# A thirteenth 8 KiB tile, w1's sums by 640 columns, and each head's gK one iteration earlier in a one-core attention block with its gradients

## The chip, the core and the metric

The kernel runs on one core of one Trainium2 chip. The metric is the device time of one execution in microseconds (us), the median of the runs. The engines are TensorE (PE in the profile; PEld is its weight load), VectorE (DVE), ScalarE (ACT), GpSimd (POOL) and SyncE (SP). SP issues the loads, POOL the stores of the two big gradients, ScalarE the stores of the weights' gradients; all of them move over the same 16 DMA engines.

## The reference

One decode step of a transformer block for 2 batch rows, and its gradients. B = 2, D = 640, 32 heads of 128, a cache of 4096 keys and values, a hidden width of 1728. All tensors are bf16.

```python
x1 = layernorm(x);  q = x1 @ wq                      # (B, 32, 128)
p  = softmax(q @ k^T * 128**-0.5);  o = p @ v        # per batch row and head, 4096 keys
h  = x + o @ wo;  x2 = layernorm(h)
out = h + relu(x2 @ w1) @ w2
# returned: out, and for a given grad_out the gradients of
# x, k_cache, v_cache, wq, wo, w1, w2
```

The caches are 64 MiB each, and so are their gradients. For each pair of batch row and head, the gradient of v (gV) is the outer product of p (4096) and the gradient of o (128); the gradient of k (gK) is the outer product of the scores' gradient and q. The scores' gradient needs dp = v times the gradient of o, so V is needed again after the whole forward pass of its batch row.

## The kernel before, in words

**Tiles.** A K or V tile of one head is 128 partitions by 8 KiB, 1 MiB. `NBIG = 12` such tiles (L80) are shared out by tag: "ld" for loads, "g" for gV and gK, "f" and "q" for later work. `take` and `give` (L89, L105) hand them out in order; `share` (L118) says how many each tag shall own. A load waits, on SP, until the last reader of the tile it takes over is done, and the loads behind it on SP wait with it. The queue of loads (L1100 to L1129) is filled in order: K of head i, V of head i - 2, later W (V for the second pass), with w1, w2 and wo between them; `pump` issues as many as there are free tiles.

**First pass.** `p1_iter(i)` (L449) works on three heads at once, in eight steps k = 0 to 7. For head i: K is transposed on TensorE (as pairs of bf16 in fp32, L423), copied to SBUF by ScalarE (L428, tiles "XT", five buffers) and multiplied by q (L436). For head i - 1: the maximum (rmax L559, spread by a product L503, reduced to nb L505), the exponential (ep, L512, its sum in `es`), and two halves of pk, K weighted by ep (L464, VectorE). For head i - 2: V weighted by the probabilities (m_ps, L457, 32 products) and a row of u (L486). The last six V tiles of batch row 0 and of batch row 1 are kept (`KEPT`, L395) for the second pass.

**Middle of a batch row.** `middle_gen(b)` (L719) runs in the background, some steps per iteration: the layer norm, the hidden layer, and the gradient that comes back. Through w1 it comes as sums of products on VectorE (`ttr`, L641, w1_t times a row spread over all partitions, `fbc`, into a scratch row `junk`): three stretches of 576 columns for each of 5 chunks, 15 sums. `bcast_cols` (L615) spreads the row, 512 columns at a time, by TensorE and a copy on ScalarE. `go_group` (L658) then forms, for up to eight heads, the gradient of o by one sum over wo_t each, and what else the heads need. `turn()` (L649) lets one sum go ahead for each place that `slot` grants.

**Second pass.** `p2_iter(j)` (L814) does head j: transposes W (tiles T0 to T3), forms dp; spreads two rows by products (L831) that ScalarE copies to `rb`; POOL copies the probabilities to `pp`; VectorE forms gV in two halves (L809) from rb and pp, POOL stores it (L871). The last quarter of dp, the scores' gradient gsp (L822) and gK (two halves at L809, stored at L850) of head j are done at the start of `p2_iter(j + 1)`.

**Order.** The plan (L1089 to L1097) runs first-pass iterations 0 to 33, then 34 to 40 beside the middle of batch row 0. From iteration 41 (`P2_AT`) to 63 every second one also runs a second-pass head; I call it heavy and the one between light. A heavy iteration takes five steps of `p2_iter` after steps k = 1, 1, 3, 4 and 6 of the first pass (`MIXED`, L1139), the light one takes the last, gV's second half with its store, after k = 1 (`REST`, L1140). From iteration 66 on only the second pass runs (heads 14 to 63), with the middle of batch row 1, the gradients of w2, w1, wo and wq (`fin_gen`) and of x (`gx_gen`) in the background. In the mixed iterations the sums have a place after k = 6, and in the light one also after k = 1 (L1217). When two pools are released, more 8 KiB tiles are made in their places.

Of the kernel before, what the change touches and what calls it, by code (L numbers as in the profile page):

```python
# [7 lines left out]
FP32 = mybir.dt.float32  # L8
# [7 lines left out]
def kernel(  # L16
# [63 lines left out]
    NBIG = 12  # L80
# [71 lines left out]
    neg_ident = const.tile([128, 128], BF16)  # L152
    nc.vector.tensor_scalar(out=neg_ident[:], in0=ident_bf[:], scalar1=-SCALE, scalar2=None, op0=ALU.mult)
# [25 lines left out]
    xr = cols.tile([4 * ND, 128], BF16)  # L179
# [96 lines left out]
    def ln_bwd(gh, xh, rstd, add, dst, nb):  # L276

        def t3(name):
            return small.tile([128, nb, ND], FP32, tag=f"lb_{name}{nb}", bufs=1, name=f"lb_{name}")
# [3 lines left out]
        mm = small.tile([128, 2, nb], FP32, tag=f"lb_mm{nb}", bufs=1, name="lb_mm")  # L283
# [5 lines left out]
        nm = small.tile([128, 2, nb], FP32, tag=f"lb_nm{nb}", bufs=1, name="lb_nm")  # L289
# [32 lines left out]
    pkp = tc.alloc_tile_pool(name="pkp", bufs=1)  # L322
    hot = pkp.tile([128, 2 * H - 1], BF16)
    nc.gpsimd.memset(hot[:], 0.0)
    nc.gpsimd.memset(hot[:, H - 1:H], 1.0)
    es = pkp.tile([128, B, H], FP32)
# [73 lines left out]
    u4 = cols.tile([128, 128], FP32)  # L400
# [14 lines left out]
    def pair_transpose(nat, g, dve=False, busy=0):  # L415
# [8 lines left out]
        t_sb = mats.tile([128, GT // 2, 128], FP32, tag="XT", bufs=5, name="t_sb")  # L424
# [24 lines left out]
    def p1_iter(i, dve_group, busy):  # L449
# [60 lines left out]
        if p is not None:  # L510
            ep = pkp.tile([128, NSC, 2], BF16, tag="ep", bufs=3, name="ep")
            nc.scalar.activation(out=ep[:], in_=p["s"][:, :, None].to_broadcast([128, NSC, 2]),  # L512
                                 func=ACT.Exp, bias=nb[:], scale=SCALE, accum_out=es[:, bp, hp:hp + 1])
            p["ep"] = ep
            p["pk"] = []
            pk_tile(0)
# [21 lines left out]
        if p is not None and hp % OG == OG - 1:  # L538

            totp = p["bank"][:, 256:256 + OG]  # L540
            nc.tensor.matmul(totp, lhsT=half_f32, rhs=es[:, bp, hp + 1 - OG:hp + 1], start=True, stop=True)
# [66 lines left out]
    def u_out(b):  # L608

        t = pst([128, H], FP32, "mid", "uc_ps")  # L610
        nc.tensor.matmul(t[:], lhsT=u4[:], rhs=fold[:], start=True, stop=True)
        nc.vector.tensor_tensor(out=Uc[:, b, :], in0=t[:], in1=rt[:, b, :], op=ALU.mult)


# [18 lines left out]
    def store_row(col_bf, n, dst):  # L633
# [3 lines left out]
        r = small.tile([16, 128], BF16, tag="orow", bufs=2, name="orow")  # L637
# [3 lines left out]
    def ttr(in0, in1, acc, width, kc=128, junk=None):  # L641
        if junk is None:
            junk = cols.tile([128, D], BF16, tag="junk", name="junk")
# [14 lines left out]
    def go_group(b, h0, h1, hbc):  # L658
# [4 lines left out]
        for k in range(n):  # L663
            yield from turn()
            ttr(wo_t[:, h0 + k, :], hbc[:], go32[:, k:k + 1], D)
# [25 lines left out]
    def mlp_out():  # L691

        ml32 = small.tile([128, ND, B], FP32, tag="ml32", bufs=1, name="ml32")
# [16 lines left out]
        ml_bf = small.tile([128, ND, B], BF16, tag="ml_bf", bufs=1, name="ml_bf")  # L710
        nc.vector.tensor_copy(out=ml_bf[:], in_=ml32[:])
        y_bf = small.tile([128, B, ND], BF16, tag="y_bf", bufs=1, name="y_bf")
# [6 lines left out]
    def middle_gen(b):  # L719
        if o_next[0] < (b + 1) * H // OG:  # L720
            o_group()
        nc.vector.tensor_reduce(out=u4[:], in_=u_bank[0][:].rearrange("p (s d) -> p d s", s=4),
# [32 lines left out]
        fbc = cols.tile([128, Dff], BF16, tag="fbc", name="fbc")  # L755
# [17 lines left out]
        hbc = cols.tile([128, D], BF16, tag="rowbc", name="hbc")  # L773
        yield from bcast_cols(one(gh1c, b), ND, lambda c: 128, hbc)
# [5 lines left out]
        for h0, h1 in bounds:  # L780
            yield from go_group(b, h0, h1, hbc)
# [3 lines left out]
    def ga_gen():  # L785

        gbc = cols.tile([128, Dff], BF16, tag="fbc", name="gbc")
# [479 lines left out]
```

## Time and profile before

| | us |
|---|---|
| median of 3 runs | 897.68 (895.79 to 898.74) |
| the profiled execution | 897.56 |
| its span, first to last instruction | 895.8 |
| busy: TensorE, VectorE, ScalarE, POOL | 739.5, 687.7, 482.6, 202.7 |

In the span 211.11 MB were read from HBM and 149.13 MB written. The page divides the span in 40 slices of 22.4 us; for each it gives the GB/s moved, and the TensorE clock that was granted as a share of full speed. A view by windows gives the same for any stretch, with each engine's busy time and its count of instructions. A view of waits says which engine waited for whom: us in total, times, the longest. In the timeline the bracket at the end of a row is the idle time before it and what ended it. Matmuls are pipelined and their ends are modelled, so a busy TensorE isn't one at its peak.

### The profile page before, as it was taken

The page shows a single profiled execution, that of the slowest core. Times are in us where ns is not written, and L with a number is a line of the kernel's source. Part 1 is how long each engine was busy: PE and PEld are TensorE (multiplying, and loading weights), DVE is VectorE, ACT ScalarE, POOL GpSimd, SP SyncE. Part 2 cuts the span into 40 slices and gives each one's busy share as a digit, 9 for nine tenths or more (in the row PEclk, how much of TensorE's full clock was granted, in tenths as well). Part 3 has the DMA queues.
Part 4 walks back from the last instruction along what each step waited for, and adds up shares of the span by engine and source line. Part 5 has one row for each costly group of instructions (what it writes and reads, how often), then busy time and mean ns, then how long its engine had stood idle before and what let it go on. Part 6 is the DMA issues. An engine that isn't in the chain of part 4 may idle for free.

```text
span 895.8 us, 24578 instructions
## 1 busy us (share of the span) xinstructions
PE 739.5 (83%) x10145; PEld 616.0 (69%) x10145; DVE 687.7 (77%) x1284; ACT 482.6 (54%) x1242; POOL 202.7 (23%) x349
## 2 busy tenths in 40 slices
PE   4999899899997997997977776877878897787593
PEld 4888788788886886886766765665657665564452
DVE  2666788777887786786877897788788679987963
ACT  1444344344554554564645777777556864466372
POOL 1343444343211110010021232222111111111111
PEclk9999999999999899897995556555566855575555
DMA  9999999999879999999999999999999999999997
GB/s 379 425 418 416 417 406 418 425 424 380 311 307 370 377 399 424 424 424 422 399 383 400 422 419 422 419 415 421 417 417 363 425 425 425 425 425 426 425 422 295
DMA packets 56288, 361.84 MB, mean 404 GB/s; under 512 B 5680, under 2 KB 11760, under 8 KB 15472
## 3 DMA queue, kind: packets, MB, share of 16 engines
q1 hardware_dynamic: 34520, 211.13, 57.9%
q0 software_dynamic: 18432, 134.23, 35.9%
q10 hardware_dynamic: 3224, 14.92, 4.0%
q8 instruction: 80, 1.31, 0.5%
q14 instruction: 32, 0.26, 0.1%
HBM read 211.11 MB, written 149.13 MB: 402 GB/s over the span
## 4 chain that ended last, share of the span: by engine, by line
PE 42%; DMA 28%; DVE 14%; ACT 9%; issue 5%; SPq 1%; POOL 0%; ACTq 0%; POOLq 0%; DVEq 0%
PE t_ps L423 18%; DMA Vt<-in_A_v_cache_dram 13%; PE m_ps L457 10%; DMA out_dram<-gK 9%; DVE gV L809 4%; ACT gV L870 3%; PE s_ps L436 3%; PE u_ps L486 3%; ACT t_sb L428 2%; PE dp_ps L436 2%; DVE gK L809 2%; DVE pk L464 2%; PE o_ps L909 2%; DMA out_dram<-gV 2%; DVE junk L644 2%
## 5 line engine op out<-in xcount | busy, mean ns | idle before, releaser
L428 ACT COPY t_sb<-t_ps 128x512 f32<-128x512 f32 x479 | 273.6, 586 | 194.7 <-PE t_ps L423 189.7
L436 PEld LDWEIGHTS <-t_sb 128*128 128x128 bf16 x4096 | 179.4, 102 | 60.5 <-ACT t_sb L428 30.4
L423 PE MATMUL t_ps<-ident_f,Wt 128*128 128x128 f32 x832 | 197.1, 386 | 2.7 <-DMA Wt<-in_A_v_cache_dram 2.4
L457 PE MATMUL m_ps<-pk,Vt 128*128 128x129 bf16 x2048 | 171.9, 222 | 16.6 <-DMA Vt<-in_A_v_cache_dram 16.0
L464 DVE TENSOR_TENSOR pk<-Kt,ep 128x2048 bf16<-128x2048 bf16 x128 | 156.5, 1223 | 33.5 <-PE m_ps L457 15.4
L809 DVE TENSOR_TENSOR gK<-rb,gsp 128x2048 bf16<-128x2048 bf16 x128 | 152.6, 1226 | 15.3 <-DMA out_dram<-gV 13.2
L423 PE MATMUL t_ps<-ident_f,Kt 128*128 128x128 f32 x1024 | 156.0, 285 | 5.7 <-DMA Kt<-in_A_k_cache_dram 5.5
L423 PEld LDWEIGHTS t_ps<-ident_f,Wt 128*128 128x128 f32 x832 | 137.0, 200 | 32.3 <-issue 25.6
L457 PEld LDWEIGHTS <-Vt 128*128 128x128 bf16 x2048 | 125.3, 99 | 47.7 <-issue 28.9
L809 DVE TENSOR_TENSOR gV<-rb,pp 128x2048 bf16<-128x2048 bf16 (+1 forms) x128 | 142.7, 1140 | 10.2 <-DMA out_dram<-gK 8.8
L474 POOL COPY pk<-ep 128x16 bf16<-128x16 bf16 x80 | 84.1, 1053 | 160.8 <-ACT ep L512 86.5
L423 PEld LDWEIGHTS t_ps<-ident_f,Kt 128*128 128x128 f32 x1024 | 113.2, 145 | 9.8 <-PE s_ps L436 4.1
L436 PE MATMUL dp_ps<-gom,t_sb 128*128 128x2 bf16 x2048 | 95.9, 168 | 20.5 <-ACT t_sb L428 20.3
L871 POOL DMA_DIRECT2D out_dram<-gV x64 | 34.2, 534 | 293.2 <-DVE gV L809 173.5
L436 PE MATMUL s_ps<-qm,t_sb 128*128 128x2 bf16 x2048 | 87.4, 164 | 1.5 <-DVE t_sb L426 1.5
L850 POOL DMA_DIRECT2D out_dram<-gK x64 | 34.0, 531 | 227.6 <-DVE gK L809 172.6
L571 ACT CAST MT<-m_ps 128x128 bf16<-128x128 f32 x64 | 17.1, 267 | 105.3 <-PE m_ps L457 105.1
L915 ACT CAST ot<-o_ps 128x512 bf16<-128x512 f32 (+3 forms) x152 | 68.0, 492 | 6.9 <-DMA out_dram<-ot 5.6
L822 DVE SCALAR_TENSOR_TENSOR gsp<-dp_ps,negdot,P_bf 128x64 bf16<-128x64 f32 x64 | 18.0, 281 | 55.8 <-PE dp_ps L436 55.7
L836 ACT ACTIVATE rb<-dp_ps,rt 128x256 bf16<-128x256 f32 x64 | 30.2, 471 | 56.9 <-PE dp_ps L831 56.8
L644 DVE CUSTOM_DVE_ANT_0 junk<-wo_t,hbc 128x640 bf16<-128x640 bf16 x64 | 52.5, 820 | 0.2
L644 DVE CUSTOM_DVE_ANT_0 gxj<-wqs,gqr 128x1024 bf16<-128x1024 bf16 x40 | 48.8, 1219 | 1.4 <-DMA wqs<-in_A_wq_dram 1.2
(200 smaller groups left out, 763.2 us busy)
## 6 DMA issues: line engine op xcount, KB each, us to landing
Kt<-in_A_k_cache_dram SPq DMA_DIRECT2D x64, 1024.0 KB, 16.5
Vt<-in_A_v_cache_dram SPq DMA_DIRECT2D x64, 1024.0 KB, 16.0
out_dram<-gV POOLq DMA_DIRECT2D x64, 1024.0 KB, 13.5
out_dram<-gK POOLq DMA_DIRECT2D x64, 1024.0 KB, 13.7
Wt<-in_A_v_cache_dram SPq DMA_DIRECT2D x52, 1024.0 KB, 12.0
wq_t<-in_A_wq_dram SPq DMA_DIRECT2D x5, 1024.0 KB, 11.9
wo_t<-in_A_wo_dram SPq DMA_DIRECT2D x4, 1280.0 KB, 19.0
wqs<-in_A_wq_dram SPq DMA_DIRECT2D x5, 1024.0 KB, 21.0
```

The costliest lines, as they stand in the source:

```text
L423: nc.tensor.transpose(t_ps[:, j, :], natf[:, 2 * cc:2 * cc + 2, :].rearrange("p c k -> p (c k)"), ident_f[:])
L428: nc.scalar.copy(out=t_sb[:], in_=t_ps[:])
L436: nc.tensor.matmul(dst[:, sc:sc + 2], lhsT=v[:, j, :, par], rhs=vecs[:, par, :], start=(par == 0), stop=(par == 1))
L457: nc.tensor.matmul(r["m"][:, 0:129], lhsT=r["V"][:, sc, :], rhs=r["pk"][sc // HALF][:, sc % HALF, 0:129], start=(sc == 0), stop=(sc == NSC ...
L464: nc.vector.tensor_tensor(out=p["pk"][k][:, :, 0:128].rearrange("p s (a two) -> p s a two", two=2), in0=p["K"][:, sl, :].rearrange("p s (a ...
L474: nc.gpsimd.tensor_copy(out=col, in_=e)
L644: nc.vector.tensor_tensor_reduce(out=junk[0:kc, 0:width], in0=in0, in1=in1, scale=1.0, scalar=0.0, op0=ALU.mult, op1=ALU.add, accum_out=acc)
L809: nc.vector.tensor_tensor(out=pairs_view(dst[:, sl, :]), in0=row.rearrange("p (a two) -> p a two", two=2)[:, None, :, :].to_broadcast([128 ...
L836: nc.scalar.activation(out=rb[:], in_=bank[:, 128:384], func=ACT.Copy, scale=rt[:, b, h:h + 1])
L850: nc.gpsimd.dma_start(out=natural(out_2, bp, hp), in_=gK[:])
L871: nc.gpsimd.dma_start(out=natural(out_3, b, h), in_=gV[:])
L915: nc.scalar.copy(out=ot[0:P, k, n0:n0 + nn], in_=o_ps[0:P, 0:nn])
```

## The change

- `NBIG` is 13. In the mixed iterations the loads own 10 tiles in place of 9, in the second pass 10 until the loads are cut to 5 (as before); from there the thirteenth is a store tile (g = 6 in place of 5).
- Its 8 KiB of each partition come from small buffers: `junk` is gone (the scratch output goes to a part of P_bf that is not yet in use, to a used part of w1_t, or beside `hbc`); `fbc`, `rowbc`, `u4` share one row `wide_row`; `es` holds 8 heads; XT has 4 buffers in place of 5, rb 3 for 4, gsp and pp 2 for 3; buffers of the last stage move to the pool `fin`, where the output row `orow` has one buffer in place of two.
- w1's sums go by 640, 640 and 448 columns, each stretch spread by `spread_some` into one of two halves of the row, with one copy.
- In the mixed iterations, where the next iteration is light, head j's last dp, gsp and gK are done in that light iteration: the last dp and gsp after k = 1, gK's halves after k = 4 and k = 6, with its store on POOL behind the second. The sum's second place moves from the light to the heavy iteration.

```diff
-    NBIG = 12
+    NBIG = 13
...
-        t_sb = mats.tile([128, GT // 2, 128], FP32, tag="XT", bufs=5, name="t_sb")
+        t_sb = mats.tile([128, GT // 2, 128], FP32, tag="XT", bufs=4, name="t_sb")
...
+    def spread_some(colsrc, c0, n, kc_of, dst):
+
+        t = pst([128, D], BF16, "bc", "bcb_ps")
+        w = 0
+        for c in range(c0, c0 + n):
+            kc = kc_of(c)
+            nc.tensor.transpose(t[:, w:w + kc], colsrc[0:kc, c:c + 1].to_broadcast([kc, 128]), ident_bf[0:kc, 0:kc])
+            w += kc
+        nc.scalar.copy(out=dst[:, 0:w], in_=t[:, 0:w])
+        return w
...
-        r = small.tile([16, 128], BF16, tag="orow", bufs=2, name="orow")
+        r = fin.tile([16, 128], BF16, tag="orow", bufs=1, name="orow")
...
-        FW = Dff // 3
-        spread_f = bcast_cols(one(ghfc, b), NF, f_kc, fbc)
-        have = 0
-        for k in range(3):
-            while have < min(Dff, (k + 1) * FW):
-                next(spread_f)
-                have += 512
-                yield
+        first_f = 0
+        for k, n in enumerate((ND, ND, NF - 2 * ND)):
+            row = fbc[:, (k % 2) * D:(k % 2 + 1) * D]
+            w = spread_some(one(ghfc, b), k * ND, n, f_kc, row)
+            yield
             for c in range(ND):
                 yield from turn()
-                ttr(w1_t[:, c, k * FW:(k + 1) * FW], fbc[:, k * FW:(k + 1) * FW], gx2p[:, c, k:k + 1], FW)
+                part = w1_t[:, c, first_f:first_f + w]
+                ttr(part, row[:, 0:w], gx2p[:, c, k:k + 1], w, part if b else later_heads())
                 yield 0.85
+            first_f += w
...
-    def p2_iter(j, busy, act=0):
+    def p2_iter(j, busy, act=0, own_gK=False):
...
-        p = S2[j - 1] if j >= 1 else None
+        p = S2.get(j - 1)
...
         yield
+        if own_gK:
+            last_dp(j, c)
         outer_half(gV, c["rb"][:, 0:128], c["pp"], 1, act)
...
         nc.gpsimd.dma_start(out=natural(out_3, b, h), in_=gV[:])
         give(gV)
+        if own_gK:
+            gsp = score_grad(j, c)
         yield
+        if own_gK:
+            gK = take("g", [128, NSC, 128], "gK")
+            outer_half(gK, c["rb"][:, 128:256], gsp, 0)
+            yield
+            outer_half(gK, c["rb"][:, 128:256], gsp, 1)
+            nc.gpsimd.dma_start(out=natural(out_2, b, h), in_=gK[:])
+            give(gK)
+            del S2[j]
+            yield
...
-    REST = {1: 1}
+    REST = {1: 1, 4: 1, 6: 1}
...
-            share(ld=KEPT[1] + 3, g=5)
+            share(ld=KEPT[1] + 4, g=5)
...
-            share(ld=5 + more, g=5 + 2 * more, f=3, q=2 + 3 * more)
+            share(ld=5 + more, g=6 + 2 * more, f=3, q=2 + 3 * more)
...
-            g2 = p2_iter(j, 0, 8 if i is None and j <= H else 0)
+            g2 = p2_iter(j, 0, 8 if i is None and j <= H else 0, i is not None and plan[n + 1][1] is None)
...
-                slot[0] = int(k == 6 or (k == 1 and j is None))
+                slot[0] = int(k == 6 or (k == 1 and j is not None))
```

`last_dp` and `score_grad` hold the lines that stood at the head of `p2_iter` (the last eight products of dp, and gsp).

More of the change, by code (lines that the diff above doesn't have):

```diff
@@ L322 @@
     pkp = tc.alloc_tile_pool(name="pkp", bufs=1)
+    neg_ident = pkp.tile([128, 128], BF16)
+    nc.vector.tensor_scalar(out=neg_ident[:], in0=ident_bf[:], scalar1=-SCALE, scalar2=None, op0=ALU.mult)
     hot = pkp.tile([128, 2 * H - 1], BF16)
@@ L399 @@
     u_bank = [None]
-    u4 = cols.tile([128, 128], FP32)
+    u4 = [None]
     S1 = {}
@@ L656, in one, with go_group @@
         return src[:, :, b]
-    def go_group(b, h0, h1, hbc):
+    def go_group(b, h0, h1, hbc, junk):
         hs = slice(h0, h1)
@@ L664, in go_group @@
             yield from turn()
-            ttr(wo_t[:, h0 + k, :], hbc[:], go32[:, k:k + 1], D)
+            ttr(wo_t[:, h0 + k, :], hbc, go32[:, k:k + 1], D, junk)
             yield 0.9
@@ L691, in mlp_out @@
     def mlp_out():
-        ml32 = small.tile([128, ND, B], FP32, tag="ml32", bufs=1, name="ml32")
+        ml32 = fin.tile([128, ND, B], FP32, tag="ml32", bufs=1, name="ml32")
         nc.vector.memset(ml32[:], 0.0)
@@ L772, in middle_gen @@
         yield from ln_bwd(gx2[:], x2c[:, :, b:b + 1], rstd2[:, b:b + 1], gc[:, :, b:b + 1], gh1c[:, :, b:b + 1], 1)
-        hbc = cols.tile([128, D], BF16, tag="rowbc", name="hbc")
-        yield from bcast_cols(one(gh1c, b), ND, lambda c: 128, hbc)
+        row = wide_row("hbc")
+        hbc, junk = row[:, 0:D], row[:, D:2 * D]
+        spread_some(one(gh1c, b), 0, ND, lambda c: 128, hbc)
+        yield
         yield ("gh1", b)
@@ L780, in middle_gen @@
         for h0, h1 in bounds:
-            yield from go_group(b, h0, h1, hbc)
+            yield from go_group(b, h0, h1, hbc, junk)
         if b > 0:
@@ L785, in ga_gen @@
     def ga_gen():
-        gbc = cols.tile([128, Dff], BF16, tag="fbc", name="gbc")
+        gbc = wide_row("gbc")
         for b in range(B):
@@ L1019, in gx_gen @@
         gxp = fin.tile([128, B, ND, NGW], FP32, tag="gxp", name="gxp")
-        junk = cols.tile([128, GW], BF16, tag="fbc", name="gxj")
+        junk = wide_row("gxj")
         for c in range(ND):
@@ L1039, in gx_gen @@
         for b in range(B):
-            gxo = small.tile([128, ND], BF16, tag="gxo", bufs=2, name="gxo")
+            gxo = fin.tile([128, ND], BF16, tag="gxo", bufs=2, name="gxo")
             nc.vector.tensor_copy(out=gxo[:], in_=gx_bf[:, :, b])
```

62 lines of the change are left out of this document (36 added, 26 removed).

## The prediction

> **What bounds the kernel now.** I read the slices of the page first: what moved, and how evenly.
>
> ```profile
> GB/s 379 425 418 416 417 406 418 425 424 380 311 307 370 377 399 424 424 424 422 399 383 400 422 419 422 419 415 421 417 417 363 425 425 425 425 425 426 425 422 295
> DMA packets 56288, 361.84 MB, mean 404 GB/s; under 512 B 5680, under 2 KB 11760, under 8 KB 15472
> ```
>
> The best slices stand at 424 to 426 GB/s and none lies above. At 424 GB/s the 361.84 MB take 361.84/0.424 = 853.4 us, and the span is 895.8 us, so 42.4 us are transfer time that wasn't used. The change moves no byte fewer; it can only win by filling those 42.4 us. Where they lie is read from the windows cut by stage (columns: window, length, busy us of each engine with its instructions, granted clock, DMA share, GB/s):
>
> ```profile
> 0.00:20.00 20.00, 8.05 (x177) 7.39 (x178) 5.91 (x42) 1.87 (x2) 3.10 (x18) 1.00 0.91 373
> 20.00:200.00 180.00, 170.68 (x2929) 149.71 (x2929) 132.58 (x241) 73.64 (x221) 74.61 (x93) 0.99 1.02 419
> 200.00:258.00 58.00, 55.41 (x973) 48.93 (x972) 46.97 (x132) 29.62 (x80) 15.43 (x28) 1.00 0.88 344
> 258.00:342.00 84.00, 76.29 (x1248) 66.53 (x1249) 68.20 (x139) 47.66 (x132) 10.23 (x15) 0.96 0.95 373
> 342.00:440.00 98.00, 86.10 (x1366) 75.75 (x1363) 72.89 (x147) 50.36 (x139) 10.09 (x17) 0.90 1.01 422
> 440.00:500.00 60.00, 46.79 (x683) 41.73 (x682) 47.51 (x96) 31.82 (x86) 11.70 (x23) 0.74 0.99 393
> 500.00:660.00 160.00, 120.03 (x1170) 97.31 (x1169) 131.55 (x233) 111.88 (x295) 41.63 (x78) 0.56 1.01 419
> 660.00:700.00 40.00, 32.89 (x345) 26.33 (x345) 31.23 (x56) 28.20 (x59) 7.00 (x15) 0.67 0.97 389
> 700.00:880.00 180.00, 141.93 (x1256) 101.21 (x1254) 146.65 (x201) 106.69 (x232) 27.79 (x60) 0.57 1.01 424
> 880.00:896.00 16.00, 1.34 (x20) 1.11 (x18) 4.17 (x5) 0.84 (x2) 1.15 (x3) 0.50 0.57 238
> ```
>
> Unused time of a stage is its length times (424 - rate)/424: 2.4 at the start, 2.1 in 20 to 200, **10.9 in 200 to 258** (the middle of batch 0), **10.1 in 258 to 342** (the first mixed iterations), 0.5 in 342 to 440, 4.4 in 440 to 500, 1.9, then 3.3 in 660 to 700, nothing in 700 to 880, 7.0 in the tail. From 342 to 440 and from 700 to 880 the transfers are the bound. In 200 to 342 they aren't: there they wait for a free tile. The DMA queue's own waits in 258 to 342, longest first (us, times, longest), start with this row, the last reader of a K tile:
>
> ```profile
> SPq L444 <- DVE pk L464: 35.8, 5, 11.8
> ```
>
> The loads that SP issues there, in order of time, are K44, V42, K45, V43, K46:
>
> ```profile
> 270.26 0.33 SPq L444 DMA_DIRECT2D Kt<-in_A_k_cache_dram  x1
> 270.68 0.74 SPq L444 DMA_DIRECT2D Vt<-in_A_v_cache_dram  x1
> 277.68 0.33 SPq L444 DMA_DIRECT2D Kt<-in_A_k_cache_dram  x1
> 279.38 0.33 SPq L444 DMA_DIRECT2D Vt<-in_A_v_cache_dram  x1
> 279.76 1.00 SPq L444 DMA_DIRECT2D Kt<-in_A_k_cache_dram  x1
> ```
>
> Between 270.68 and 277.68 nothing is issued. TensorE then reaches V43 before it has landed, and its clock falls (timeline of TensorE, then windows):
>
> ```profile
> 286.11 1.06 PE L423 MATMUL t_ps<-ident_f,Kt 128*128 128x128 f32 x8 [0.86 <-DMA Kt<-in_A_k_cache_dram]
> 287.01 0.22 PE L503 MATMUL s_ps<-neg_ident,rmax 128*128 128x128 bf16 x1
> 290.04 0.64 PE L457 MATMUL m_ps<-pk,Vt 128*128 128x129 bf16 x8 [2.81 <-DMA Vt<-in_A_v_cache_dram]
> ```
>
> ```profile
> 287.00:291.00 4.00, 1.05 (x19) 0.76 (x18) 0.46 (x4) 0.85 (x2) 0.00 (x0) 0.98 1.02 424
> 291.00:296.00 5.00, 4.76 (x46) 4.63 (x45) 3.77 (x5) 2.64 (x8) 0.53 (x1) 0.50 1.01 426
> 296.00:302.00 6.00, 6.00 (x93) 4.87 (x91) 3.55 (x7) 3.09 (x8) 0.00 (x0) 0.86 0.74 288
> ```
>
> The reason is in the code: six V tiles of batch 0 are kept for the second pass, so only 12 - 6 = 6 tiles turn over for loads.
>
> **The change part by part.**
>
> *The thirteenth tile.* Each load from here on takes the place that the load after it had: V43 goes out where K45 stood, at 277.68 and not at 279.38, and K45 has left 7.00 us earlier and no longer shares the way with it. While engines set the pace, one tile more doesn't raise the rate (each iteration frees two tiles either way); it lets the transfers run 1 MiB further ahead before they stop. That is 1.049/0.424 = 2.5 us, once for each stretch that lies between two transfer-bound ones. For 200 to 342, which I count as one stretch, I take **-2.5**. Bounds: 0, if the transfers aren't the bound later, and -2.5.
>
> *The wait for V43.* 0.86 + 2.81 = 3.7 us of idle TensorE, and behind it 5 us at 0.50 and 6 us at 0.86 of the clock, at most 2.5 + 0.8 = 3.3 us of TensorE's work. V43 starts 1.7 us earlier with one load less ahead of it, so most of the wait goes.
>
> *Each head's gK in the light iteration.* From iteration 41 on every second iteration is heavy: it also transposes a W tile and forms gV's first half. A pair of iterations (heavy and light) loads 4 tiles and stores 2 up to the sixth head, then loads 5. At 424 GB/s that is 6 x 1.049/0.424 = 14.8 us, later 17.3. The Exp of heads 40 and 48, four pairs apart:
>
> ```profile
> 258.49 0.32 ACT L512 ACTIVATE ep<-s_ps,nb 128x64 bf16<-128x64 f32 x1
> ...
> 324.96 0.32 ACT L512 ACTIVATE ep<-s_ps,nb 128x64 bf16<-128x64 f32 x1
> ```
>
> 66.5 us for four pairs, 16.6 each, against 14.8: at most 66.5 - 59.3 = 7.2 us are to be had before the transfers bind. VectorE's groups in 258 to 342 price its share (columns: busy, mean ns, idle before):
>
> ```profile
> L464 DVE TENSOR_TENSOR pk<-Kt,ep 128x2048 bf16<-128x2048 bf16 x21 | 25.7, 1226 | 5.9 <-PE m_ps L457 5.0 <-issue 0.7
> L644 DVE CUSTOM_DVE_ANT_0 junk<-wo_t,hbc 128x640 bf16<-128x640 bf16 x15 | 12.3, 817 | 0.0
> L809 DVE TENSOR_TENSOR gV<-rb,pp 128x2048 bf16<-128x2048 bf16 x10 | 12.2, 1217 | 0.0
> L809 DVE TENSOR_TENSOR gK<-rb,gsp 128x2048 bf16<-128x2048 bf16 x10 | 11.8, 1222 | 0.2
> L505 DVE TENSOR_REDUCE nb<-s_ps 128x1 f32<-128x128 f32 x11 | 3.2, 287 | 0.5 <-PE s_ps L503 0.5
> L559 DVE TENSOR_REDUCE rmax<-s_ps 128x1 bf16<-128x32 f32 x10 | 1.9, 191 | 2.7 <-PE s_ps L436 2.7
> L547 DVE COPY P_bf<-ep 128x32 bf16<-128x32 bf16 x10 | 1.8, 179 | 0.0
> L822 DVE SCALAR_TENSOR_TENSOR gsp<-dp_ps,negdot,P_bf 128x64 bf16<-128x64 f32 x5 | 1.4, 282 | 4.4 <-PE dp_ps L436 4.3
> ```
>
> Two pk halves, nb, rmax and P_bf are 2 x 1.226 + 0.287 + 0.191 + 0.179 = 3.1 us in each iteration. Before, the heavy one adds three outer halves, gsp and one sum: 3.1 + 3.66 + 0.28 + 0.82 = 7.9; the light one a half and two sums: 3.1 + 1.22 + 1.63 = 6.0. After it is the other way round, since the second sum's place moves to the heavy iteration too: 6.0 and 7.9. The pair stays at 13.9, under 14.8. What moves is the coupling: in the heavy iteration TensorE has the 16 more transposes (two rows of 8 in 1.06, 2.1 us), and VectorE's long turn no longer coincides with them; and gsp, which stood at the head of the heavy iteration with 4.3 us of waiting for dp in five heads, is formed where nothing of the next W tile hangs on it. Of what is added to the light iteration, POOL's gK store moves too: it now goes out behind gV's and ahead of the next head's pp, which isn't needed until the heavy iteration's end. For wait and levelling together I take **-4.5** of the 7.2 (the 3.7 and 0.8 more); bounds: +6.8 (rival B) and -7.2.
>
> *Dips further on.* In 440 to 500, where loads also queue for tiles, the extra tile can cover 2.5 of 4.4; the slices of 399, 383 and 400 GB/s make that up, and I take **-1.5** (bounds 0 and -2.5). In 20 to 200 and 660 to 700, 2.1 + 3.3 are unused; loads are cut to five tiles ahead of the second one in both kernels, and the thirteenth goes to the stores. I take **-0.5** (bounds 0 and -3.5).
>
> *w1 sums by 640 columns.* In 210 to 258 the row of the 15 sums by 576 is
>
> ```profile
> L644 DVE CUSTOM_DVE_ANT_0 junk<-w_t,fbc 128x576 bf16<-128x576 bf16 x15 | 11.3, 755 | 0.5 <-ACT fbc L625 0.3
> ```
>
> Ten at 817 and five of 448 columns (estimate from 755 and 817: 62 ns for 64 columns, so 631) are 8.2 + 3.2 = 11.3: **0**. ScalarE copies three rows instead of four. Bounds -0.5 and +0.5. The scratch outputs in P_bf and w1 are written where a scratch row was written, at the same price.
>
> *Small buffers.* XT with 4 in place of 5 suffices because a head's last transposed tile is now used in the light iteration's second stage. The output row has one buffer in place of two, so VectorE's second copy (both now back to back) waits until the first has been stored. This is at
>
> ```profile
> 783.68 0.86 SPq L639 DMA_DIRECT2D out_dram<-orow  x2
> ```
>
> With VectorE waiting, gK and gV of the next head are behind it. In 740 to 790 a store takes from issue to landing, by the DMA view,
>
> ```profile
> out_dram<-gK POOLq DMA_DIRECT2D x6, 1024.0 KB, 32.2
> out_dram<-gV POOLq DMA_DIRECT2D x5, 1024.0 KB, 32.0
> Wt<-in_A_v_cache_dram SPq DMA_DIRECT2D x4, 1024.0 KB, 20.1
> ```
>
> so some 32 us of stores stand queued and cover a wait of up to that; the small store, on the loads' queue, should land within their 20. I take 0; without that cover it would be up to +20.
>
> Sum: -2.5 - 4.5 - 1.5 - 0.5 = -9.0. The profiled execution took 897.56 us (1.8 around its span) and the median of the runs shown is 897.68. 897.56 - 9.0 = **888.5 us**.
>
> The Trainium skill speaks against such a gain: "DMA: Bandwidth & Descriptors", section "Where 436 GB/s comes from", says that for transfers between HBM and SBUF the HBM side binds at about 358 GB/s. By it 200 to 258 would have had 58 x 14/358 = 2.3 us to fill and 258 to 342 none, and the time would be about 895 (an estimate from that page). The trace doesn't bear it out, with 424 GB/s over the 180 us from 700 on, and so it gets no chance of its own.
>
> **The rivals.** *A: the dip belongs to the engines.* In 200 to 258 TensorE is busy 55.4 of 58 us, in 258 to 342 76.3 of 84. If the pairs stay at 16.6 the tile gives only its lead, with or without the later dips: 895.1 to 893.6. For it: the same two rows. Against it: the wait at 290 and the empty queue before it.
> *B, the slower side: the light iteration becomes VectorE's.* TensorE's share of a pair is (76.3 - 3.3) x 16.6/84 = 14.4, the 3.3 for the slow clock; with 2.1 more in the heavy one that is 8.3 and 6.2. If the iterations can't overlap, before costs max(7.9, 8.3) + max(6.0, 6.2) = 14.5 and after 8.3 + 7.9 = 16.2: +1.7 a pair, 6.8 over the four pairs, and, at 16.6 + 1.7 = 18.3 against 17.3, 1.0 in each of seven more. Less the 2.5 of the lead and the 3.7 of the wait: 897.6 + 13.8 - 6.2 = 905; with only the four pairs hit, 898. It decides from a pair of 17.3 us on. Against it: VectorE and TensorE are coupled by three pk tiles, one and a half heads' worth, and VectorE's pair is 13.9.
> *C: the dip fills whole.* All the bounds: -2.5 - 7.2 - 2.5 - 3.5 = -15.7: 882.
> *D: the tile doesn't reach the loads* (turned over to stores, or late): 897.6. Against it: in the changed program's order each K and V load stands one place earlier from the first iterations on.
>
> **How the numbers follow.** Forecast (884 to 893): 0.56. C (879 to 884): 0.14. A: 0.14, half of it under 894.9. B: 0.10. D: 0.06 (its 897.6 is no change). A measurement of this kernel tells 0.3%, 2.7 us, from no change. So faster 0.56 + 0.14 + 0.07 = 0.77, same 0.07 + 0.06 = 0.13, slower 0.10. The range from 880.5 to 896.5 takes in the forecast, most of C, and A; B and D are left out.
>
> **What would show it.** Right: 373 GB/s in the first mixed stage becomes over 400, no wait of over 1 us for a V tile near head 43, a pair of 15 to 15.5 us, 342 to 440 unchanged in shape but some 7 us earlier. Wrong: pairs of 16.6 or more, with VectorE's light turn as the releaser of TensorE's m_ps or of K tiles; stores of gV and gK waiting for tiles in the mixed stage; VectorE standing at the output row for more than the queued stores cover; a fall of the clock to 0.5 in the mixed stage.

## The result and the profile after

The changed kernel takes 891.21 us (median of 22 runs, 889.45 to 896.39) against 897.59 (22 runs, 893.36 to 904.16): a ratio of 0.9934, 95% interval 0.9921 to 0.9948. The forecast was 888.5 in a range from 880.5 to 896.5. The profiled execution took 890.62 us, 6.9 below that of before; its span is 888.8.

The slices of the page:

```profile
GB/s 378 424 419 415 417 408 416 426 423 414 336 309 357 424 423 424 424 425 424 416 386 398 416 420 424 415 415 420 418 423 412 419 425 421 425 424 423 410 374 314
DMA packets 56288, 361.84 MB, mean 407 GB/s; under 512 B 5680, under 2 KB 11760, under 8 KB 15472
```

The packets are the same to the last one. The dip behind 200 us is three slices under 400 GB/s long in place of six, the slices from 290 to 400 are full, and two slices shortly before the end have become worse (410 and 374 for 425 and 422). The windows by stage (window, length, busy us of PE, PEld, DVE, ACT, POOL with their instructions, granted clock, DMA share, GB/s):

```profile
20.00:200.00 180.00, 172.55 (x2929) 151.60 (x2929) 133.03 (x241) 73.52 (x221) 74.78 (x93) 0.99 1.02 419
200.00:258.00 58.00, 55.18 (x970) 48.70 (x969) 47.22 (x133) 29.02 (x78) 15.57 (x28) 1.00 0.93 361
258.00:342.00 84.00, 78.74 (x1348) 69.17 (x1347) 70.53 (x142) 51.26 (x140) 6.69 (x15) 1.00 0.97 393
342.00:440.00 98.00, 82.76 (x1335) 73.01 (x1333) 73.53 (x150) 51.29 (x140) 7.83 (x18) 0.95 1.01 424
440.00:500.00 60.00, 45.90 (x666) 40.85 (x664) 46.40 (x92) 33.15 (x88) 11.86 (x26) 0.72 0.99 394
660.00:700.00 40.00, 33.59 (x430) 29.25 (x428) 32.16 (x52) 29.50 (x57) 8.31 (x18) 0.71 1.01 417
700.00:880.00 180.00, 138.77 (x1143) 97.37 (x1142) 141.81 (x197) 101.18 (x223) 26.34 (x56) 0.54 0.99 410
880.00:888.80 8.80, 0.00 (x0) 0.00 (x0) 1.18 (x2) 0.00 (x0) 0.53 (x1) 0.50 0.58 244
```

Unused time by the prediction's own formula, length times (424 - rate)/424, before and after:

| stage | before | after | difference | forecast |
|---|---|---|---|---|
| 200 to 440 | 21.5 | 14.7 | -6.8 | -7.0 |
| 440 to 500 | 4.4 | 4.2 | -0.2 | -1.5 |
| 20 to 200 and 660 to 700 | 5.4 | 2.8 | -2.6 | -0.5 |
| 700 to the end of the span | 6.9 | 9.6 | +2.7 | 0 |

Together -6.9, the difference of the two profiled executions. In this pair of executions the big term came nearly whole, the next one didn't come, and the end lost what nobody had charged to it. How far such a row can be trusted is shown by eight of the experiments below, whose edits act only from iteration 66 on: with the same code as the changed kernel up to there, they have 14.1 to 20.1 us unused in 200 to 440.

The big term by its own signs: the Exp of heads 40 and 48 (timeline of ScalarE),

```profile
258.82 0.32 ACT L513 ACTIVATE ep<-s_ps,nb 128x64 bf16<-128x64 f32 x1
...
319.44 0.32 ACT L513 ACTIVATE ep<-s_ps,nb 128x64 bf16<-128x64 f32 x1 [0.50 <-DVE nb L506]
```

are 60.6 us apart, 15.15 a pair, where they were 66.5 and 16.6. This sign is firm: in the eight other profiles of the same code the four pairs take 60.1 to 60.8. What scatters is when head 40 comes, from 258.6 to 264.5 with the same code, so some executions lose up to 6 us ahead of the mixed iterations.

The loads took the places that the prediction gave them. Here are V42, K45 and V43:

```profile
270.89 0.33 SPq L445 DMA_DIRECT2D Vt<-in_A_v_cache_dram  x1
271.31 0.38 SPq L445 DMA_DIRECT2D Kt<-in_A_k_cache_dram  x1
278.01 0.33 SPq L445 DMA_DIRECT2D Vt<-in_A_v_cache_dram  x1
```

K45 leaves 6.4 us earlier than before, and V43 goes out where K45 stood. The view of TensorE's waits from 200 to 342 has no row left that names a load; before it had V43's 2.8 and K's 0.9. The clock of the first mixed stage is 1.00 instead of 0.96.

At the end, VectorE's second copy of an output row and SyncE's row beside it (timeline):

```profile
769.52 0.21 DVE L657 COPY orow<-row_ps 5x128 bf16<-5x128 bf16 x1
783.21 0.21 DVE L657 COPY orow<-row_ps 5x128 bf16<-5x128 bf16 x1 [13.48 <-DMA out_dram<-orow]
```

```profile
769.79 13.94 SPq L658 DMA_DIRECT2D out_dram<-orow  x2
783.83 0.79 SPq L445 DMA_DIRECT2D Wt<-in_A_v_cache_dram  x1
```

The single output row holds VectorE for 13.5 us, and SyncE with it: its second store waits for the second copy, and the loads of W stand behind that store.

### The profile page after: what moved, and what is told of

It is laid out like the page before. It is cut to its first block, busy times and chain, and to the rows that moved or that the text cites. A ratio compares the mean times of both kernels' runs of the same rounds, so it can differ in the third digit from the quotient of the medians.

```text
span 888.8 us, 24680 instructions
## 1 busy us (share of the span) xinstructions
PE 737.0 (83%) x10145; PEld 615.2 (69%) x10145; DVE 685.5 (77%) x1284; ACT 483.8 (54%) x1238; POOL 198.7 (22%) x349
## 4 chain that ended last, share of the span: by engine, by line
PE 38%; DMA 25%; DVE 21%; ACT 8%; issue 7%; SPq 1%; ACTq 0%; POOL 0%; POOLq 0%; DVEq 0%
PE t_ps L424 16%; DMA Vt<-in_A_v_cache_dram 13%; PE m_ps L458 8%; DVE gK L828 5%; DMA out_dram<-gK 5%; DVE gxj L661 5%; DVE gV L828 4%; PE s_ps L437 3%; ACT gV L902 3%; DVE pk L465 3%; DMA wqs<-in_A_wq_dram 2%; PE u_ps L487 2%; PE dp_ps L437 2%; ACT t_sb L429 2%; DMA out_dram<-orow 1%
## 5 line engine op out<-in xcount | busy, mean ns | idle before, releaser
L458 PE MATMUL m_ps<-pk,Vt 128*128 128x129 bf16 x2048 | 170.8, 221 | 17.9 <-DMA Vt<-in_A_v_cache_dram 15.2
L880 POOL DMA_DIRECT2D out_dram<-gK x53 | 28.2, 531 | 141.3 <-DVE gK L828 112.6
L661 DVE CUSTOM_DVE_ANT_0 hbc<-wo_t,hbc 128x640 bf16<-128x640 bf16 x64 | 53.0, 828 | 0.3
## 6 DMA issues: line engine op xcount, KB each, us to landing
Kt<-in_A_k_cache_dram SPq DMA_DIRECT2D x64, 1024.0 KB, 17.3
```

Source lines behind the costliest of these rows:

```text
L458: nc.tensor.matmul(r["m"][:, 0:129], lhsT=r["V"][:, sc, :], rhs=r["pk"][sc // HALF][:, sc % HALF, 0:129], start=(sc == 0), stop=(sc == NSC ...
L661: nc.vector.tensor_tensor_reduce(out=junk[0:kc, 0:width], in0=in0, in1=in1, scale=1.0, scalar=0.0, op0=ALU.mult, op1=ALU.add, accum_out=acc)
L880: nc.gpsimd.dma_start(out=natural(out_2, bp, hp), in_=gK[:])
```

## The experiments

Twelve kernels ran, each beside the kernel before on the same chip; ratios are to that kernel and carry their intervals. All unused times are worked out from one profiled execution each.

### Was it the tile or the place of gK?

The changed kernel with 12 tiles (**own_only**), and with 13 tiles but gsp and gK back at the head of the next heavy iteration (**gk_heavy**):

```diff
-    NBIG = 13
+    NBIG = 12
...
-            share(ld=KEPT[1] + 4, g=5)
+            share(ld=KEPT[1] + 3, g=5)
...
-            share(ld=5 + more, g=6 + 2 * more, f=3, q=2 + 3 * more)
+            share(ld=5 + more, g=5 + 2 * more, f=3, q=2 + 3 * more)
```

```diff
-    REST = {1: 1, 4: 1, 6: 1}
+    REST = {1: 1}
...
-                slot[0] = int(k == 6 or (k == 1 and j is not None))
+                slot[0] = int(k == 6 or (k == 1 and j is None))
...
-        if own_gK:
-            gsp = score_grad(j, c)
...
```

> The changed kernel with 12 tiles (9 for loads in the mixed iterations, 5 for stores later). Theory: the tile gives its lead (2.5 us) and most of the wait for V43 (3.7): 895 to 898, with a wait for V of over 1 us and a pair of 16 us or more in the first mixed stage. Rival: the gain is the levelling of the mixed iterations: 891 to 893, pairs of 15.2.

> The changed kernel with gsp and gK back at the head of the next heavy iteration and the sums' places as before; only the last eight products of dp stay in the light iteration (four XT buffers need that). Theory: the tile carries the gain: 891 to 893, pairs of 15.2 to 15.8 and no wait for V. Rival: the levelling carries it: 895 to 897, pairs of 16 or more.

And with neither (**gk_heavy12**, both edits), to close the square:

> The changed kernel without its thirteenth tile and without the move of gK into the light iteration: what is left of the change is the small buffers, the w1 sums by 640 columns and the order of the REST slots. With the runs that had one of the two (tile alone 892.9, gK alone 898.4, both 891.2 to 891.5) it closes the square. Theory (the rest is worth nothing; the tile carries the gain and the move is worth at most 1.5 beside it): 897.5 to 900, and a head pair of the mixed stage takes 16.2 to 16.8 us as before. Rival (the rest has a price of its own that the two cover): 901 or more. Second rival (the two only add): 899.5 to 900.5.

| | 12 tiles | 13 tiles |
|---|---|---|
| gK in the next heavy iteration | 899.0, 1.0014 (0.9986 to 1.0042) | 892.87, 0.994 (0.9917 to 0.9964) |
| gK in the light iteration | 898.4, 1.0009 (0.9988 to 1.003) | 891.21, 0.9934 (0.9921 to 0.9948) |

The upper left corner is the time of before: small buffers and w1's sums cost nothing that can be measured (its interval reaches from -1.3 to +3.8 us), as forecast. The tile alone is worth 0.74%, 6.6 us; the move alone 0.05%, and beside the tile 0.06%, both far inside the noise. Yet the move does something. The windows of own_only, which has no thirteenth tile:

```profile
258.00:342.00 84.00, 78.09 (x1339) 68.36 (x1337) 69.90 (x141) 50.50 (x137) 6.69 (x15) 1.00 0.96 393
342.00:440.00 98.00, 82.09 (x1317) 72.14 (x1318) 74.12 (x151) 51.04 (x139) 7.83 (x18) 0.95 1.01 425
440.00:500.00 60.00, 46.90 (x648) 42.09 (x646) 43.72 (x87) 31.70 (x85) 10.56 (x23) 0.67 0.95 373
700.00:880.00 180.00, 140.26 (x1220) 100.00 (x1219) 141.63 (x196) 105.65 (x228) 27.56 (x59) 0.55 1.00 411
```

The first mixed stage runs at 393 GB/s as in the changed kernel, and its four pairs take 61.4 us. With the tile alone they take 60.4, with both 60.1 to 60.8 (nine profiles), with neither 64.9. Either edit takes that stage nearly all the way; they are alternatives there and not terms to be added. What own_only wins there (373 to 393 GB/s, 4.0 us) is not in its time. In its one profile it is lost again at 440 to 500, where 7.2 us are unused and not 4.4, and after 700; that the time is that of before is measured, where it goes back is read from this one execution.

### What is a tile worth?

**tiles11**: two tiles fewer than the changed kernel, the loads' share down by one at each stage against 12.

```diff
-    NBIG = 13
+    NBIG = 11
...
-            share(ld=KEPT[1] + 4, g=5)
+            share(ld=KEPT[1] + 2, g=5)
...
-            share(ld=5 + more, g=6 + 2 * more, f=3, q=2 + 3 * more)
+            share(ld=4 + more, g=5 + 2 * more, f=3, q=2 + 3 * more)
```

> The changed kernel with 11 tiles of 8 KiB instead of 13 (the loads' share goes down by one at each stage against 12). Theory (a tile is lead time for the loads, and its worth falls as dips fill): the step from 11 to 12 costs at least what the step from 12 to 13 gained, 7, so 905 to 915, with the mixed stage 258 to 342 below 385 GB/s. Rival (the thirteenth tile pays only because it happens to lift one threshold, as in the share given at the change of pass): 897 to 901, the same as with 12.

923.07 us, 1.0282 (1.0246 to 1.0318): even more than the first theory said. From 11 to 12 a tile is worth 24.7 us (to own_only), from 12 to 13 it is 7.2. Windows, and the first row of TensorE's waits in 200 to 342 (us, times, longest), tiles11 and then before:

```profile
200.00:258.00 58.00, 52.35 (x935) 46.09 (x932) 43.32 (x116) 26.89 (x74) 16.37 (x27) 1.00 0.78 300
258.00:342.00 84.00, 69.20 (x1083) 59.71 (x1080) 58.85 (x128) 40.90 (x112) 6.61 (x16) 0.90 0.86 322
440.00:500.00 60.00, 45.93 (x668) 40.57 (x665) 42.08 (x87) 24.84 (x65) 6.11 (x15) 0.84 0.91 351
```

```profile
PE m_ps L458 <- DMA Vt<-in_A_v_cache_dram: 16.4, 8, 4.7
PE m_ps L457 <- DMA Vt<-in_A_v_cache_dram: 3.2, 2, 2.8
```

The three dips that lack tiles deepen (17, 20 and 10 us unused), and the wait that before had twice comes eight times. In the changed kernel TensorE is busy 78.74 of 84 us in the mixed stage and waits for no load, so I'd expect a fourteenth tile to find little there; that wasn't run.

### Does a tile help at the change of pass?

440 to 500 is where the forecast's 1.5 us didn't come. **share5** and **share3** leave the number of tiles alone and shift one between loads and stores from iteration 66 on:

```diff
-            share(ld=KEPT[1] + 4, g=5)
+            share(ld=KEPT[1] + 5, g=4)     # share5
+            share(ld=KEPT[1] + 3, g=6)     # share3
```

> The changed kernel with one tile more for loads and one less for stores from the change of pass on (the share of loads 11 in place of 10, of stores 4 in place of 5). 440 to 500 had been forecast to gain 1.5 from the tile and still has 4.2 us unused. Theory 1 (loads still lack tiles there): 440 to 500 has under 3 us unused, 889 to 890.5. Theory 2 (the loads there wait for heads whose pace TensorE and VectorE set at the change of pass, so a tile more only lets the transfers run ahead once more): 440 to 500 as before, 890.5 to 892. Rival (stores then lack tiles: gK and gV wait for places to come free): 893 to 900.

> The other way: 9 tiles for loads and 6 for stores from the change of pass on, which is the loads' share of the kernel before, with the extra tile given to stores there. Theory 1 (loads lack tiles there): 440 to 500 has 6 us or more unused, 893 to 896. Theory 2 (the engines set the pace there): 890.5 to 892.5. Rival (stores lacked tiles): 887 to 890.

share3: 893.09, 0.9951 (0.9927 to 0.9975). share5: 897.17, 0.9995 (0.9973 to 1.0018); the whole gain is gone. Windows of share5, and behind them those of share3:

```profile
440.00:500.00 60.00, 44.46 (x651) 39.75 (x651) 43.97 (x91) 31.68 (x84) 11.77 (x24) 0.74 1.01 414
500.00:660.00 160.00, 121.61 (x1161) 99.23 (x1161) 129.22 (x230) 110.91 (x289) 45.25 (x75) 0.52 1.00 412
660.00:700.00 40.00, 32.22 (x362) 27.27 (x362) 35.20 (x61) 26.99 (x53) 11.64 (x20) 0.62 0.96 385
```

```profile
440.00:500.00 60.00, 45.91 (x657) 41.11 (x656) 45.77 (x92) 32.62 (x86) 11.73 (x26) 0.70 0.94 375
500.00:660.00 160.00, 125.59 (x1209) 101.33 (x1207) 135.03 (x246) 115.26 (x300) 47.02 (x77) 0.55 1.01 419
660.00:700.00 40.00, 34.09 (x354) 29.02 (x354) 29.14 (x43) 27.19 (x55) 7.01 (x15) 0.64 1.01 421
```

In 440 to 500 itself the three profiles step as theory 1 asked: with 9, 10 and 11 tiles for loads 6.9, 4.2 and 1.4 us are unused. But the scatter is as large as a step. Eight profiles with 10 tiles have 3.4 to 6.5, four with 9 (before, own_only, gk_heavy12 and share3) 4.4 to 7.2; their means are 4.7 and 5.9. Only share5's 1.4 lies clear of the rest. And the stores that lose a tile seem to pay: in share5 VectorE's gV stands and waits for a store to leave its place (VectorE's groups, 500 to 880; share5, the changed kernel, and gk_heavy):

```profile
L828 DVE TENSOR_TENSOR gV<-rb,pp 128x2048 bf16<-128x2048 bf16 x90 | 99.0, 1130 | 11.8 <-DMA out_dram<-gV 10.6 <-ACT t_sb L429 1.1
```

```profile
L828 DVE TENSOR_TENSOR gV<-rb,pp 128x2048 bf16<-128x2048 bf16 x92 | 101.4, 1132 | 3.1 <-DMA out_dram<-gK 3.1
```

```profile
L828 DVE TENSOR_TENSOR gV<-rb,pp 128x2048 bf16<-128x2048 bf16 x92 | 101.4, 1132 | 14.4 <-DMA out_dram<-gK 13.6 <-ACT ot L948 0.7
```

500 to 700 has 8.2 us unused where the changed kernel has 2.6, and the stretch from 700 on 12.4 instead of 9.6. Won 2.8, lost 5.6 and 2.8: 5.6 us in all, against 6.0 between the medians. (The two profiled executions are 9.8 apart; 3.7 of that lie in 200 to 440, ahead of the edit.) The time is in the rival's 893 to 900, and since only the shares differ, the loss comes from taking a tile from the stores. That VectorE's wait is how it comes about isn't shown: gk_heavy has a longer one (the last row), with 5.9 us unused in 500 to 700, at 892.87.

share3 also bears on the square. It gives the loads from iteration 66 on no more tiles than own_only has, and is still 5.3 us faster. So most of the tile's worth lies elsewhere, in the loads ahead of iteration 66 or in the further store tile behind it; no run here separates these two.

### The wait for the output row

**orow2** gives each row a place of its own in a part of P_bf that has been used up; **orow_act** leaves one row and stores it from ScalarE's queue.

```diff
-        r = fin.tile([16, 128], BF16, tag="orow", bufs=1, name="orow")
-        nc.vector.tensor_copy(out=r[0:n, :], in_=t[0:n, :])
-        nc.sync.dma_start(out=dst, in_=r[0:n, :])
+        r = P_bf[0:n, 4 * b:4 * b + 4, :].rearrange("p h s -> p (h s)")
+        nc.vector.tensor_copy(out=r, in_=t[0:n, :])
+        nc.sync.dma_start(out=dst, in_=r)
...
```

```diff
-        nc.sync.dma_start(out=dst, in_=r[0:n, :])
+        nc.scalar.dma_start(out=dst, in_=r[0:n, :])
```

> The changed kernel, with two places for the output row again (a used part of P_bf). Theory: VectorE's wait of 13.5 us for the first row's store used up the queued stores and held SP's loads, and the transfers run dry at the end for it (394 GB/s in 820 to 830, 306 to 374 in 855 to 875): without it no wait there, and 3 us less than the changed kernel, about 888. Rival: the end runs dry because the engines end there anyway: the wait goes, the time stays within 1 us of 891.

> The changed kernel, its one output row stored from ScalarE's queue in place of SP's. Theory: the small store took 13.5 us because it lay behind loads on SP's queue, and SP's next loads stood behind the second one: VectorE's wait falls under 5 us, SP isn't held, the time is that of two rows, about 888. Rival: a store of any size takes that long beside 32 us of queued stores: the wait stays over 10 us, and since SP goes on loading, between 889 and 891.

orow2: 892.18, 0.9939 (0.9914 to 0.9963). orow_act: 892.02, 0.9947 (0.9923 to 0.9971). The wait is gone in one and 5.2 us in the other, and neither is faster than the changed kernel. My first theory, 3 us for the wait, fell. The windows around it show what became of it; the changed kernel, then orow2:

```profile
760.00:790.00 30.00, 15.20 (x114) 9.80 (x114) 16.38 (x27) 10.09 (x24) 2.77 (x6) 0.50 1.01 424
840.00:880.00 40.00, 35.09 (x283) 24.49 (x282) 26.22 (x31) 26.70 (x54) 6.29 (x14) 0.50 0.90 374
```

```profile
760.00:790.00 30.00, 20.68 (x146) 13.02 (x146) 29.43 (x47) 13.57 (x33) 5.34 (x11) 0.50 1.01 427
840.00:880.00 40.00, 31.17 (x254) 21.62 (x254) 25.36 (x29) 24.10 (x49) 7.59 (x15) 0.50 1.01 424
```

While VectorE stands, the transfers go on at 424; the hole comes 60 to 90 us later, when the stores that weren't formed are missing. All twelve kernels that move all the bytes bear that out: the six with a wait of 12.4 us or more have 1.7 to 4.8 us unused in 840 to 880, the six with 10.0 us or less (before among them, which has none) 0 to 0.9 (for tiles11, which is some 30 us later as a whole, in 870 to 910). Without the wait that hole is filled, but the end is slow. In orow2 the last store is issued at 877.24 and the span ends at 892.4; its last 16 us, in 40 slices of 0.4 us (DMA view):

```profile
GB/s 471 379 451 420 461 430 379 451 430 430 440 440 410 369 481 328 328 328 184 225 225 102 164 61 61 20 20 41 20 20 41 20 20 41 0 0 0 0 0 0
```

In the 3.6 us before the last packet lands, 2.1 us ahead of the end of the span, about 27 GB/s move, a sixteenth of 424: 8 KB packets of 0.31 us one behind the other, as one of the 16 DMA engines would move them (the trace names no engine). A single packet at a time is in flight for 0.4 us in the changed kernel, for 3.8 in orow2 and for 2.6 in orow_act (worked out from the packets' records). Here too the twelve kernels part in the same way: the six with a hole in 840 to 880 run out for 0.3 to 1.4 us, the six without one for 1.9 to 5.8. So what is won by filling the hole is paid back, in part at least, at the run-out.

### Whose is the run-out?

**orow2_sync** is orow2, and **sync_last** the changed kernel, with the eight gV and gK stores of heads 60 to 63 issued by SyncE:

```diff
-        nc.gpsimd.dma_start(out=natural(out_3, b, h), in_=gV[:])
+        (nc.sync if j >= 60 else nc.gpsimd).dma_start(out=natural(out_3, b, h), in_=gV[:])
...
```

> The changed kernel with two places for the output row, in which in addition the gV and gK stores of the second pass's heads 60 to 63 are issued by SyncE, whose loads have all been issued by then, instead of GpSimd. In the run with two places alone the transfers fill 424 GB/s from 700 to 880, yet the time is the same (892.2); its last 4 us move 28 GB/s, the packets of one DMA engine out of 16 one after the other, all of them of GpSimd's stores, and the landing records say that the 16 parts of such a store land 8 to 10 us apart from 780 on, while those of SyncE's loads lie 2.5 to 6 us apart. Theory: it is GpSimd's queue whose parts have drifted apart, and what was won at 770 to 783 is paid back while its slowest part runs out; the last eight stores on the other queue then end with the rest: 887 to 889.5, with at most 2 us at under 60 GB/s at the end. Rival: the engine itself is behind with everything it is given, whatever queue it comes from: 891 to 893, and 4 us or more at under 60 GB/s.

> The changed kernel with nothing but the issue of the gV and gK stores of heads 60 to 63 moved from GpSimd to SyncE. Its single output row starves the loads around 860 to 880, and its profiled run ended without the long run-out of one engine (under 100 GB/s for the last 2 us only). Theory (GpSimd's queue drifts apart in the saturated stretch, a dip lets it catch up): little left to win here, 889.5 to 891.5. Rival (the stores start later or earlier from another queue, whatever the run-out): the same gain or loss as in the kernel with two places for the row.

orow2_sync: 892.76, 0.9954 (0.9927 to 0.9981); sync_last: 891.11, 0.9914 (0.9887 to 0.9941), not to be told from the changed kernel. orow2_sync is no clean test, since VectorE waited 19 us for places of the stores there and the last store went out only at 885.5; its run-out is 1.9 us. sync_last is one: its last 16 us, by the DMA view, with the queues that had packets in them (q0, GpSimd's, had its last one at 868.8):

```profile
GB/s 451 440 461 358 461 420 348 451 461 440 379 389 430 410 502 420 379 440 471 420 358 154 154 113 92 113 41 20 20 41 20 20 41 20 20 20 0 0 0 0
...
q1 hardware_dynamic: 436, 3.16, 47.0%
q10 hardware_dynamic: 203, 0.73, 11.2%
q8 instruction: 1, 0.02, 0.4%
```

Not a packet of GpSimd's, and the run-out of one engine is there, 3.4 us of it, in SyncE's stores. The theory of GpSimd's queue falls as it was put: the engine that is behind is behind with whatever it is given. Why it is, and whether GpSimd's packets up to 868.8 had put it behind, no run here shows.

### What bounds the end?

**less** is the changed kernel and **orow2_less** is orow2 with four of gK's stores left out:

```diff
-            nc.gpsimd.dma_start(out=natural(out_2, bp, hp), in_=gK[:])
+            if not 56 <= j - 1 < 60:
+                nc.gpsimd.dma_start(out=natural(out_2, bp, hp), in_=gK[:])
```

> The changed kernel without the four stores of gK of the heads 56 to 59 of the second pass (gK is computed, 4 MiB of the third output are not written), issued between about 815 and 855 us; at 424 GB/s they take 9.9 us. It measures what bounds the end. Theory: in the changed kernel the last 20 us are set by the chain of heads (a head every 7 to 8 us, gsp at 871.5 and 878.5, then gK and its store), the transfers having dips at 855 to 875 already, so that dropped bytes only leave longer dips: 887 to 890. Rival (the transfers, saturated up to 855, still set the end): the 9.9 us come off nearly whole, 881 to 884.

> The same four stores left out (4 MiB of the third output are not written) of the kernel with two places for the output row, whose heads end 4 to 9 us earlier (gsp at 874.3 in a run that had lost 5 us before 260) while its last store lands 15 us after its issue. Theory (there the transfers set the end and the heads lie about 5 us ahead): 883 to 887, so 3 us or more below the changed kernel without the same stores; this is the 3 us that the wait for the row would have cost, had the transfers not covered it. Rival (the wait is worth nothing in either, both ends are set by the same thing): the two kernels without the stores agree within 1.5 us.

less: 887.68, 0.9862 (0.9841 to 0.9883). orow2_less: 882.93, 0.9837 (0.9807 to 0.9868). Of 9.9 us of transfers left out, 9.2 come off orow2. Off the changed kernel 3.5 come by the medians and 6.5 by the ratios to before; the six runs of less lie from 885.28 to 893.64. The two kernels are 4.8 us apart by the medians, as the theory asked, and 2.2 by the ratios, between the theory and its rival, and the intervals overlap. The times lean to the theory and don't settle it. The windows; less, then orow2_less:

```profile
700.00:840.00 140.00, 102.09 (x873) 72.72 (x872) 115.08 (x160) 73.93 (x170) 18.46 (x39) 0.57 0.99 412
840.00:888.00 48.00, 36.44 (x288) 25.02 (x286) 29.15 (x39) 28.27 (x57) 6.52 (x15) 0.50 0.73 302
```

```profile
700.00:840.00 140.00, 109.58 (x1015) 77.61 (x1015) 123.64 (x171) 83.39 (x188) 21.73 (x44) 0.60 1.01 424
840.00:888.00 48.00, 35.09 (x283) 24.52 (x282) 28.59 (x37) 27.01 (x55) 7.79 (x15) 0.50 0.84 348
```

From 700 to the end of the span 20.7 us are unused in less and 9.2 in orow2_less. They point the same way, but more weakly than they look: the two profiled executions, 892.82 and 890.49 us, are 5.1 and 7.6 above their kernels' medians, and orow2_less had lost 9 us more ahead of 700, so that more was left to transfer behind it. The likeliest reading is that the changed kernel ends with two bounds almost side by side: the heads, which the wait delays, and the transfers with their run-out. Take bytes away, and the heads set the end (less); take the wait away, and the transfers do (orow2), at the same time. It isn't shown beyond doubt.

## Why the prediction was right, and where it wasn't

**The bound and the place: right.** No byte less moved, and the gain is dips that were filled. K45 and V43 go out where the prediction put them, V43's wait is gone, and a pair takes 15.15 us in the forecast 15 to 15.5, and 15.0 to 15.2 in every profile of this code. From head 40's Exp to head 63's it takes 189.7 us in place of 195.8, and 188.4 to 191.9 in the eight other profiles, so 3.9 to 7.4 of the 7 us forecast. That 200 to 440 gave 6.8 of the 7.0 is closer than one pair of executions can tell, with 14.1 to 20.1 unused by the same code: the size is right, the closeness luck. 258 to 342 stayed a little under the 400 GB/s that were asked for, at 393.

**How that term was divided: wrong.** It was the sum of 2.5 for the tile's lead and 4.5 for the wait and the levelling, as if they were two things. The square shows them as two ways to the same 60 to 61 us for four pairs, of which only the tile's way lasts to the end: 6.6 us against 0.4. The 4.5 of the sum counted what the levelling gains in its stage as gained for good, and that step failed: own_only's pairs are 1.3 us shorter each than before's, and its time is the same.

**440 to 500: not seen.** "The extra tile can cover 2.5 of 4.4", taken as 1.5, came to 0.2 in the two profiled executions. The means over all profiles, 5.9 us unused with 9 tiles for loads and 4.7 with 10, are 1.2 apart, near the forecast; but each group's scatter, 4.4 to 7.2 and 3.4 to 6.5, is larger than that, and whether this term was right stays open. The dip may also grow when the first pass comes to it earlier: 6.9 and 7.2 with 9 tiles in share3 and own_only, whose pairs are short, 4.4 and 5.1 in before and gk_heavy12, whose pairs are long. Four single profiles lean to it and don't show it.

**20 to 200 and 660 to 700:** the first didn't move (419 GB/s in both); 660 to 700 gained 2.6. It isn't the tile's for certain: single profiles of the kernels with 12 tiles show 0.4, 1.8 and 3.3 there, those with 13 from 0.3 to 3.7.

**The small buffers: the number right, the reason only half.** I charged 0 to the output row because 32 us of queued stores would cover VectorE. They covered it while it stood; the missing stores then made a hole at 840 to 880. It costs nothing that can be measured: orow2 and orow_act, without the hole, end no earlier. And SyncE, which queues loads behind the row's second store, was overlooked; for 13.94 us the W loads stood behind it.

**The end: unforeseen.** 2.7 us more are unused from 700 on: 5.9 more up to 880, 3.2 less behind it. In the twelve kernels that move all the bytes, before and after among them, this stretch has 6.5 to 12.4 us unused, in no order by tile or queue; the step that failed is that I charged the end nothing and gave it no range. Against the forecast of -9.0 the profiled -6.9 is made up so: 0.2 less in 200 to 440, 1.3 less in 440 to 500, 2.7 lost at the end, 2.1 more than forecast in 660 to 700. That the misses nearly cancel is luck, and each is read from one pair of executions.

**The rivals.** A (dips of the engines) would have left the pair at 16.6: it fell with 15.15. B fell with the same row: it asked for 17.3 or more. C asked for 9.7 us in 200 to 440 and got 6.8; 14.7 stay unused there, all in 200 to 342. D fell: K45's lead is there and nothing waits for loads. The changed kernel moves 424 GB/s over the 98 us from 342 to 440. That decides again against the rule of the Trainium skill, "DMA: Bandwidth & Descriptors", section "Where 436 GB/s comes from" (358 GB/s on the HBM side).

## What to carry to other kernels

Where transfers bound most of a kernel and stall in a few places, count the unused transfer time by stage: an edit is worth what remains of it at the end of the run, not in its own stage. Here a buffer more kept its worth to the end, and levelling an iteration, which helped its stage nearly as much, did not. And take such a count from several profiled executions before a term of a few us is believed: the same code left 14.1 to 20.1 us unused in one stretch.

## What the runs showed of the hardware

A store of 1.2 KB took 13.5 us (8.5 to 14.3 in eight other kernels that left it there) to give its buffer back when it was issued on SyncE's queue, 11 us behind a 1 MiB load, and 5.2 us from ScalarE's queue at the same place in the program. On SyncE's queue at 851 us in sync_last, with no load issued for 25 us, such a store took 4.9.

After a stretch at 424 GB/s the transfers didn't all finish together. In the six kernels with at most 0.9 us unused in the 40 us from 840 on (tiles11 from 870 on), 8 KB packets run out one at a time, at about 27 GB/s, for 1.9 to 5.8 us (3.0 in before, 3.8 in orow2, 3.4 in sync_last); in the six with a hole there, for 0.3 to 1.4. They did so whichever queue the last stores came from. The Trainium skill, "DMA: Bandwidth & Descriptors", section "Latency and other measured facts", says that two of the 16 engines are usually slower in traces, and guesses at the descriptor rings of GpSimd's queue as the cause. That some engine ends later agrees with the run-outs; the trace doesn't name it. In sync_last it ended as late with no packet of GpSimd's for 20 us, so such packets needn't be there at the end; whether they had put the engine behind earlier, no run here shows.
